# A list scheduler inside a spectral-mixing and expert-retrieval kernel: new transfer costs, work taken by latest time, and six instead of seven units by block products

## The chip, the cores and the metric

The kernel runs on one core of one Trainium2 chip. The metric is the device time of one launch in microseconds (us). The matrix engine (TensorE) is PE in the profile, and its weight loads, which overlap the products, are PEld; VectorE is DVE, ScalarE is ACT, GpSimd is POOL, SyncE is SP. SP does no arithmetic here: its instructions issue DMA transfers, one after the other, and an instruction that waits for a semaphore holds up all those behind it.

## The reference

Two layers follow each other, and each does two steps on x, which has 2048 rows (tokens) of 512 numbers:

```python
x = x + A(layernorm(x))     # a = xn @ Wd_re.T; b = xn @ Wd_im.T; A = Ws_re @ a - Ws_im @ b
x = x + B(layernorm(x))     # q = xn @ w_q (32 heads); scores of q's halves against k1 and k2 (16 keys each);
                            # the best two of each half -> the best two of their four pairs -> softmax g;
                            # out = sum over heads and picks of g * gelu(xn . u[pick]) * v[pick]
```

A is a Fourier transform over tokens and features, of which only the real part is kept: Ws has 2048 x 2048 numbers (real and imaginary part), Wd 512 x 512. B looks up 2 of 256 experts for each of the 32 heads of each token.

## The kernel before, in words

**Numbers.** Each float32 operand of a product is split in two float16 words, a high one (by ACT) and a rest (by DVE), and a product is three matmuls: high by high, rest by high, high by rest. The matrices `c` (from the sequence matrix), `xh`/`xl` (the normalised rows), `dh`/`dl` (the hidden matrix) and `wh`/`wl` (w_q folded with the keys) are such pairs.

**Units.** A layer's A step goes over nine units of output tokens: units 0 to 6 have 256 tokens (two tiles of 128), units 7 and 8 have 128 each. A unit first does the sequence product: for pairs of token tiles `p0` it loads two pieces of the sequence matrix (`raw`, 256 KB each), makes the pair `c`, and multiplies with all of `xh`/`xl` into the accumulators `acc`. `seq_unit` (L899 on) does this directly: 192 matmuls of 512 columns for a unit of 256 tokens, at L1054. `fast_unit` (L717 to L896) does it by block products in the manner of Strassen: seven products in place of eight, 336 matmuls of 256 columns at L815. For this, DVE forms sums of blocks of `raw` (L750, L754, L758), ACT and DVE split 1024 and 768 columns per step instead of 1024, and the sums are stored in DRAM (`sum2d`, L788) and read back as `m` (L884); at the end DVE and ACT join the products (L838, L853). Which units are fast is the table `FAST`, one tuple for each layer. Fast units of layer 0 also store `c` (`sum1d`, L791), and a unit that is fast in both layers loads it in layer 1 (L732 on) and prepares nothing.

**Token tiles.** When a unit's sequence product is complete, each of its tiles goes through `token_tile` (L1082 on): 24 matmuls with `dh`/`dl` (L1162), the row is added and normalised again (L289, L327 to L340), split (`xp`), turned by a transposing DMA (`xt`, L1193), multiplied for scores (L1276, L1281) and for u (L1313); DVE finds the best keys (L1368 to L1411), a second turn (`qd`, L1193) and comparisons with `iota` make one-hot factors `lr`; 32 small matmuls (L1670) sum the softmax weights; four DMAs to DRAM and two back (`gdr`, L1740, L1747) rearrange them; after a weighing by the activations the product is turned (`pl`, L1193) and multiplied by v (L1815, L1819). In layer 0 the row is stored in DRAM (`x2d`, L1870) and read again in layer 1. All these transfers are issued by SP. The last tile of layer 1 takes a path of its own ("fine"), with PE transpositions and shorter pieces, because nothing follows it.

**Order.** Nothing runs in the order of the code. Each step is recorded as an operation of one engine (`Plan.op`, L90) with an assumed duration, the operations it must follow (`after`), those it must merely stand behind (`behind`), the buffers that it takes and frees (`Hold`), and a priority `prio`. `Plan.run` (L97) is a list scheduler: it keeps a clock for each engine, and of the operations that can start first on an engine it takes the one with the least `prio`. The start times give the order in which each engine's instructions are emitted; on the chip each engine then runs its own list in that order and waits by semaphores. A load occupies SP for its whole transfer (`load(kb)` is 1.05 us for 256 KB) and lands `lag` 2.3 us later; a transposing DMA is `TURN, TURNED = 1.2, 1.4`. In the tail, after the last sequence product, PE is fed idle matmuls (`fill`, L2021) where the plan has a gap of over 0.8 us: they keep it running and compute nothing.

**Set-up.** In the first 160 us w_q is loaded in 32 pieces of 512 KB (`wr`, L529), split (`w`, L603, L271) and folded with the keys by small matmuls (L617, L619), between the sequence products of units 0 to 2. No tile can have its scores before that is complete.

## Time and profile before

| quantity | value |
|---|---|
| three runs | 1168.27, 1174.51, 1174.88 us (median 1174.51) |
| the profiled execution: its time, its span | 1169.87 us, 1168.1 us |
| PE busy, share of the span | 1114.9 us, 95% |
| DVE busy | 1008.0 us, 86% |
| ACT busy | 624.8 us, 53% |
| POOL busy | 56.4 us, 5% |
| the transfers of SP's queue: share of the 16 DMA engines | 58.3% (187.54 MB) |

The page's first part gives busy times, of which the largest is the first guess at a bound. Idle time counts only on the engine that sets the end; on the others it is slack. A wait row reads "engine, line waited for, the engine and line that ended the wait: us in total, times, the longest". A row of the windows view gives, for a stretch of the span, busy us and number of instructions of each engine, the share of full speed that TensorE's clock was granted (PEclk), and the DMA engines' busy share and rate. Rows of the chain and of the timeline begin with start and duration in us. Consecutive matmuls overlap: a 512-column matmul has 379 ns on its own row, and the next starts 216 ns after it, so a rate is read from a run of them.

### The profile page before, as it was taken

How to read it: one execution, taken by the hardware profiler on the slowest of the kernel's cores; microseconds unless marked ns; L12 is line 12 of the kernel's file. 1: busy time of each engine (PE TensorE's matmuls, PEld its weight loads, DVE VectorE, ACT ScalarE, POOL GpSimd, SP SyncE). 2: the span in 40 equal slices, each digit the busy share in tenths (PEclk: the TensorE clock that was granted, in tenths of full speed). 3: DMA queues.
4: the chain of work that ended last, by engine and by line, in shares of the span. 5: the costliest groups of instructions: out<-in, count | busy, mean ns of one | idle time of the engine just before them, and what ended most of it. 6: DMA issues, size and time to landing. Idle time of an engine off the chain costs nothing.

```text
span 1168.1 us, 21993 instructions
## 1 busy us (share of the span) xinstructions
PE 1114.9 (95%) x8350; PEld 687.0 (59%) x8350; DVE 1008.0 (86%) x2048; ACT 624.8 (53%) x1200; POOL 56.4 (5%) x106
## 2 busy tenths in 40 slices
PE   8999999989999879999999999999999899999996
PEld 3345544444458556766645644667776666667574
DVE  8768879998799998989896589999999977988696
ACT  6666666566555465556654575654644345344322
POOL 2100000001000000000000000000000000000000
PEclk9999999999999999999999999999999999999998
DMA  8688764455367877644536442787687765454111
GB/s 275 200 265 270 252 214 107 129 131 132 105 178 237 197 240 196 198 108 104 157 97 145 152 113 90 209 214 204 203 211 238 176 164 131 126 107 112 32 29 31
DMA packets 307587, 189.16 MB, mean 162 GB/s; under 512 B 193424, under 2 KB 267408, under 8 KB 307472
## 3 DMA queue, kind: packets, MB, share of 16 engines
q1 hardware_dynamic: 307328, 187.54, 58.3%
q8 instruction: 67, 1.10, 0.4%
q14 instruction: 48, 0.39, 0.1%
q10 hardware_dynamic: 144, 0.13, 0.0%
HBM read 137.77 MB, written 36.57 MB: 149 GB/s over the span
## 4 chain that ended last, share of the span: by engine, by line
PE 48%; DVE 29%; DMA 11%; ACT 4%; issue 4%; SPq 3%; POOL 1%; DVEq 0%; ACTq 0%
PE acc L1054 13%; PE acc L815 10%; PE bank L1162 9%; PE bank L1276 5%; DVE c L271 4%; PE bank L1281 3%; DVE eq L1390 3%; DMA raw<-in_cseq 3%; DVE eq L1368 2%; DMA xt<-xp 2%; PE bank L1313 2%; DVE lr L1634 2%; DVE tmp L1374 2%; DVE tmp L1381 1%; PE bank L1815 1%
## 5 line engine op out<-in xcount | busy, mean ns | idle before, releaser
L1054 PE MATMUL acc<-c,xh 128*128 128x512 f16 (+1 forms) x1232 | 327.1, 346 | 3.3 <-DVE ptl L271 2.2
L1054 PE MATMUL acc<-c,xl 128*128 128x512 f16 (+1 forms) x616 | 213.0, 346 | 1.9 <-DVE xl L405 1.9
L1054 PEld LDWEIGHTS <-xh 128*128 128x128 f16 x1360 | 133.0, 98 | 106.8 <-DVE ptl L271 2.2
L277 ACT ACTIVATE c<-raw 128x1024 f16<-128x1024 f32 (+1 forms) x120 | 118.9, 995 | 67.5 <-PE acc L1054 26.4
L271 DVE SCALAR_TENSOR_TENSOR c<-raw,c 128x1024 f16<-128x1024 f32 (+1 forms) x120 | 137.3, 1148 | 11.8 <-ACT c L277 10.9
L1162 PE MATMUL bank<-dh,pth 128*128 128x512 f16 (+1 forms) x264 | 97.7, 373 | 0.5 <-ACT pth L277 0.5
L815 PEld LDWEIGHTS <-xch 128*128 128x128 f16 x896 | 88.5, 99 | 15.6 <-DMA m<-sum2d 2.2
L1054 PEld LDWEIGHTS <-xl 128*128 128x128 f16 x680 | 66.5, 98 | 52.9 <-DVE xl L405 3.0
L1162 PE MATMUL bank<-dl,pth 128*128 128x512 f16 (+1 forms) x264 | 97.6, 373 | 0.0
L1162 PE MATMUL bank<-dh,ptl 128*128 128x512 f16 (+1 forms) x264 | 92.6, 373 | 0.0
L1276 PE MATMUL bank<-wh,xt 128*128 128x512 f16 x216 | 82.0, 380 | 10.6 <-DMA xt<-xp 10.4
L815 PE MATMUL acc<-c,xh 128*128 128x256 f16 x448 | 85.6, 274 | 6.7 <-ACT c L277 3.3
L1390 DVE SCALAR_TENSOR_TENSOR eq<-eq 128x512 f16<-128x512 f16 x186 | 86.1, 463 | 1.0
L815 PE MATMUL acc<-m,xch 128*128 128x256 f16 x448 | 79.6, 276 | 6.2 <-DMA m<-sum2d 6.2
L815 PE MATMUL acc<-c,xch 128*128 128x256 f16 x448 | 85.1, 275 | 0.0
L1162 PEld LDWEIGHTS <-pth 128*128 128x128 f16 x528 | 50.9, 98 | 52.9 <-ACT pth L277 0.6
L1276 PE MATMUL bank<-wl,xt 128*128 128x512 f16 x216 | 81.9, 379 | 0.0
L1634 DVE TENSOR_TENSOR lr<-iota,qt 128x2048 f16<-128x2048 f16 x58 | 69.5, 1219 | 10.7 <-ACT qt L1601 9.8
L1368 DVE TENSOR_TENSOR eq<-sc,val 128x1024 f16<-128x1024 f32 x62 | 75.8, 1223 | 1.4
L1276 PEld LDWEIGHTS <-xt 128*128 128x128 f16 x432 | 41.1, 98 | 60.5 <-DMA xt<-xp 14.2
L815 PEld LDWEIGHTS <-xh 128*128 128x128 f16 x672 | 65.9, 98 | 13.3 <-issue 3.3
L1281 PE MATMUL bank<-wh,xt 128*128 128x512 f16 x248 | 63.6, 379 | 0.0
(243 smaller groups left out, 2208.8 us busy)
## 6 DMA issues: line engine op xcount, KB each, us to landing
raw<-in_cseq SPq DMA_DIRECT2D x192, 256.0 KB, 3.5
m<-sum2d SPq DMA_DIRECT2D x84, 256.0 KB, 3.6
wr<-in_wq SPq DMA_DIRECT2D x32, 512.0 KB, 5.8
sum2d<-s SPq DMA_DIRECT2D x40, 384.0 KB, 3.5
sum1d<-c SPq DMA_DIRECT2D x16, 512.0 KB, 3.7
raw<-in_ctile SPq DMA_DIRECT2D x32, 256.0 KB, 3.7
c<-sum1d SPq DMA_DIRECT2D x16, 512.0 KB, 4.3
e<-x2d SPq DMA_DIRECT2D x30, 256.0 KB, 3.0
```

The costliest lines, as they stand in the source:

```text
L271: nc.vector.scalar_tensor_tensor(lo, src, scale, hi, op0=ALU.mult, op1=ALU.subtract)
L277: nc.scalar.activation(hi, src, AF.Copy, scale=scale)
L815: nc.tensor.matmul(acc[m][:, dd], w(pw, dd), moving(pm), start=(first and dd == 0 and k == 0), stop=(j == half_t - 1 and dd == 1 and k == ...
L1054: nc.tensor.matmul(target(d), w[:, s, d * P:(d + 1) * P], moving(s % per, part), start=(s == 0 and k == 0 and d % blocks == 0), stop=(s == ...
L1162: nc.tensor.matmul(t["y", cs.start], w[:, k, c, t0:t0 + P], r[:, c, k, cs], start=(z == 0 and c == 0 and m == 0), stop=(z == len(steps) - ...
L1276: nc.tensor.matmul(t["pc", hf], t["th"][:, k, :], r[:, k, hf], start=(k == 0 and r is wh), stop=False, skip_group_check=fine)
L1281: nc.tensor.matmul(t["pc", hf], t["tl"][:, k, :], wh[:, k, hf], start=False, stop=(k == KD - 1), skip_group_check=fine)
L1313: nc.tensor.matmul(t["xu"], w[:, k, :], r[:, k, :], start=(m == 0), stop=(m == 3 * KD - 1))
L1368: nc.vector.tensor_tensor(t["eq"][:, :, cols], flat("sc")[:, :, cols], val(rank_, cols), op=ALU.is_equal)
L1374: nc.vector.tensor_max(t["tmp"][:, :, cols], flat("sc")[:, :8, cols], flat("sc")[:, 8:, cols])
L1390: nc.vector.scalar_tensor_tensor(s[:, :m], s[:, :m], 2.0 ** m, s[:, m:2 * m], op0=ALU.mult, op1=ALU.max)
L1634: nc.vector.tensor_tensor(both(r), iota[:, :, 0:4][:, None, :, :].to_broadcast([P, 32, E, 4]), rows(r), op=ALU.is_equal)
```

## The change

The change has four parts.

- **Costs.** A transfer now has three numbers: the time for which it occupies its issuer, its share of a common pipe, and a tail until it has landed. `load` becomes 0.5, 0.98 us per 256 KB, 1.55; the new `store` 0.48, 0.84 per 256 KB, 1.05; the transposing DMA of `xt` 1.3, 1.55, 1.4, those of `qd` and `wt` (the `pl` row) 1.3, 0.65, 1.4; the `gdr` transfers 0.7, 0.13, 1.6 and 0.7, 0.96, 1.5. Transfers pass the common pipe one after the other.
- **Choice.** The plan is made 8 times. After each pass, `latest` works a latest start for every operation back from the start times of PE's operations, every second time with PE's operations packed without gaps; in the next pass DVE, ACT, POOL and SP take the operation with the least latest time. PE still goes by `prio`. The pass with the earliest end is kept.
- **Units.** `FAST` goes from ((5, 6), (2, 3, 4, 5, 6)) to ((6,), (1, 2, 3, 5, 6)): six block-product units instead of seven. Unit 4 is a direct unit in both layers; layer 0 stores its `c` (`keptd`, L1079 of the new program) and layer 1 loads it, without a split by ACT and DVE. The order of layer 1's units goes from 0, 7, 1, 2, 3, 4, 5, 6, 8 to 0, 7, 4, 3, 6, 1, 2, 5, 8.
- **Queue and small waits.** The `x2d` stores of layer 0 are issued by ACT instead of SP. Some operations get a further predecessor (`last[i][0]`, `p_place`, `first_m`, `setup_done`) which their data needs or which stood ahead anyway.

```diff
-FAST = ((5, 6), (2, 3, 4, 5, 6))
+FAST = ((6,), (1, 2, 3, 5, 6))
+KEPT = (4,)
...
+        self.issue = None
+        if isinstance(us, tuple):
+            self.issue, us, lag = us
...
+    def best(self, passes):
+        found, due = None, None
+        for k in range(passes):
+            out = self.run(due)
+            end = max(o.end for o in out)
+            if found is None or end < found[0]:
+                found = end, [(o.start, o) for o in out]
+            due = self.latest(out, k % 2)
...
+    def latest(self, out, packed):
...
+        for o in sorted(out, key=lambda o: o.start):
+            if o.engine == "PE":
+                t = due[o.n] = o.start if t is None or not packed else t
+                t += o.us
+        for o in sorted(out, key=lambda o: -o.start):
+            own = o.us + o.lag + (o.issue or 0.0)
+            d = min([t + 3.0 - own] + [due[n] - (own if whole else 0.0) - 0.1 for n, whole in follow.get(o.n, ())])
+            due[o.n] = min(due.get(o.n, d), d)
...
-                    t, o = min((c for c in can if c[0] <= first + 1e-9), key=lambda c: (c[1].prio, c[1].n))
+                    key = (lambda c: (c[1].prio, c[1].n)) if due is None or e == "PE" else (lambda c: (due[c[1].n], c[1].n))
+                    t, o = min((c for c in can if c[0] <= first + 1e-9), key=key)
...
-            free[e] = t + max(o.us - self.OVER.get(e, 0.0), 0.06 if o.us else 0.0)
-            o.end = t + o.us + o.lag
-            if o.lag:
+            if o.issue is None:
+                free[e] = t + max(o.us - self.OVER.get(e, 0.0), 0.06 if o.us else 0.0)
+                o.end = t + o.us + o.lag
+            else:
+                free[e] = t + o.issue
+                moved = max(moved, t + BEGIN) + o.us
+                o.end = moved + o.lag
...
-TURN, TURNED = 1.2, 1.4
+BEGIN = 0.55
+ROUND = (0.7, 0.13, 1.6), (0.7, 0.96, 1.5)
+TURN = {"xt": (1.3, 1.55, 1.4), "qd": (1.3, 0.65, 1.4), "wt": (1.3, 0.65, 1.4)}
...
 def load(kb):
-    return kb / 256 * 1.05
+    return 0.5, kb / 256 * 0.98, 1.55
+
+
+def store(kb):
+    return 0.48, kb / 256 * 0.84, 1.05
...
-    ORDER = ([0, 1, 2, 3, 4, 5, 6, 7, 8], [0, 7, 1, 2, 3, 4, 5, 6, 8])
+    ORDER = ([0, 1, 2, 3, 4, 5, 6, 7, 8], [0, 7, 4, 3, 6, 1, 2, 5, 8])
...
+            if layer and n in KEPT:
+                def f4():
+                    t["c"] = two_words()
+                    nc.sync.dma_start(t["c"][2], kept_d[KEPT.index(n), p0 // 2])
...
-            moves.append(op("SP", 0.3, f_out, evac[1:], behind=moves[:1], take=[hd] if k == 0 else [], last=[hgs], prio=prio,
-                            lag=2.4))
+            moves.append(op("SP", ROUND[0], f_out, evac[1:], behind=moves[:1], take=[hd] if k == 0 else [], last=[hgs], prio=prio,
+                            ))
...
-            back.append(op("SP", 0.4, f_in, moves + [a_act], behind=back, take=[hgt] if j == 0 else [], last=[hd], prio=prio, lag=3.5))
+            back.append(op("SP", ROUND[1], f_in, moves + [a_act], behind=back, take=[hgt] if j == 0 else [], last=[hd], prio=prio))
...
-        x2done[i] = op("SP", load(256), lambda: nc.sync.dma_start(x2d[i], t["row"]), [a],
-                       last=[] if keep else [hrow], prio=prio, lag=2.3)
+        x2done[i] = op("ACT", store(256), lambda: nc.scalar.dma_start(x2d[i], t["row"]), [a],
+                       last=[] if keep else [hrow], prio=prio)
...
-    order = sorted(plan.run(), key=lambda o: o.start)
+    order = plan.best(8 if narrow else 1)
```

What moves shows only in the emitted lists. Counted over the whole program, PE has 192 more matmuls of 512 columns with `acc`, 336 fewer of 256 columns, and 38 idle matmuls in the tail instead of 22; DVE has four fewer joins `e<-e,acc` and the same number of splits; SP has 16 fewer `x2d` stores (ACT has them), 12 fewer loads of `m`, and 8 stores and 8 loads of `keptd` in the place of 8 and 8 of `sum1d`.

Three places follow, each first as it was. **SP's queue at the end of the set-up** (`wr` is a piece of w_q, `raw` one of the sequence matrix, of which 56 stand ahead of the last w_q piece before, and 50 now):

```order
L529 DMA wr<-in_wq 128x2x512 x7
L972 DMA raw<-in_cseq 128x2x256 x2
L529 DMA wr<-in_wq 128x2x512
L972 DMA raw<-in_cseq 128x2x256 x2
L529 DMA wr<-in_wq 128x2x512 x3
L972 DMA raw<-in_cseq 128x2x256 x2
L529 DMA wr<-in_wq 128x2x512
L972 DMA raw<-in_cseq 128x2x256 x2
L529 DMA wr<-in_wq 128x2x512
```

```order
L585 DMA wr<-in_wq 128x2x512
L1187 DMA row<-in_x 128x512 x2
L585 DMA wr<-in_wq 128x2x512 x2
L1040 DMA raw<-in_cseq 128x2x256 x2
L585 DMA wr<-in_wq 128x2x512 x3
L1040 DMA raw<-in_cseq 128x2x256 x2
L585 DMA wr<-in_wq 128x2x512 x6
L1040 DMA raw<-in_cseq 128x2x256 x2
L585 DMA wr<-in_wq 128x2x512 x2
```

The w_q pieces come with fewer `raw` loads between them, and the last one comes after six fewer of those.

**SP's queue in layer 0, among the token tiles** (`x2d<-row` stores a finished row, the transposing DMAs turn `xp`, `q` and `ph`):

```order
L1193 DMA_TRANSPOSE qd<-q 128x3x128
L744 DMA raw<-in_cseq 128x2x256 x2
L1193 DMA_TRANSPOSE pl<-ph 128x4x128
L1870 DMA x2d<-row 128x512
L1114 DMA row<-in_x 128x512
L791 DMA sum1d<-c 128x2048
L1870 DMA x2d<-row 128x512
L1193 DMA_TRANSPOSE xt<-xp 128x8x128
```

```order
L1266 DMA_TRANSPOSE qd<-q 128x3x128
L1820 DMA g_3062<-gdr 64x16x16 x2
L505 DMA e_3077<-in_x 128x512
L505 DMA e_3084<-in_x 128x512
L1040 DMA raw<-in_cseq 128x2x256 x2
L1187 DMA row<-in_x 128x512
L1079 DMA keptd<-c 128x2048
L1266 DMA_TRANSPOSE pl<-ph 128x4x128
L1266 DMA_TRANSPOSE xt<-xp 128x8x128
```

Before, a turn could stand behind two row stores; now there are none in SP's queue, and the new store of `c` stands there.

**DVE in the tail**, where the last tile's row is normalised (`stats`, `picks`, `xn`) beside the work of the tile ahead of it (`lr`, `eq`):

```order
L346 BN_AGGR stats<-e_13887 128x2
L349 TENSOR_SCALAR stats<-stats 128x1
L352 TENSOR_SCALAR picks<-stats 128x1
L355 TENSOR_SCALAR picks<-picks 128x1
L1206 TENSOR_SCALAR xn<-row,stats,picks 128x256
L358 TENSOR_SCALAR stats<-stats,picks 128x1
L1206 TENSOR_SCALAR xn<-row,stats,picks 128x256
L1390 SCALAR_TENSOR_TENSOR eq<-eq 128x128
```

```order
L402 BN_AGGR stats<-e_13714 128x2
L1722 TENSOR_TENSOR lr<-iota,qt 128x1024
L405 TENSOR_SCALAR stats<-stats 128x1
L1722 TENSOR_TENSOR lr<-iota,qt 128x1024
L408 TENSOR_SCALAR picks<-stats 128x1
L1732 TENSOR_TENSOR lr<-lr,qt 128x1024
L411 TENSOR_SCALAR picks<-picks 128x1
L1722 TENSOR_TENSOR lr<-iota,qt 128x1024
L1279 TENSOR_SCALAR xn<-row,stats,picks 128x256
L414 TENSOR_SCALAR stats<-stats,picks 128x1
L1732 TENSOR_TENSOR lr<-lr,qt 128x1024
L1279 TENSOR_SCALAR xn<-row,stats,picks 128x256
```

The six `lr` instructions of the tile ahead stood behind the normalisation; now five stand between the row's sum and the first `xn` (one of them ahead of the rows shown), and the sixth ahead of the second.

More of the change, by code (lines that the diff above doesn't have):

```diff
@@ L115, in run @@
                     names = [h.pool for h in o.take]
-                    spare = [(sorted(self.pools[n]), names.count(n)) for n in set(names)]
+                    spare = [(sorted(x[0] for x in self.pools[n]), names.count(n)) for n in set(names)]
                     if all(len(p) >= c for p, c in spare):
@@ L150, in run @@
                              (u.late if a.engine != "PE" else 0.0) for a in u.after] +
-                            [a.start + a.us for a in u.behind])
+                            [a.start + (a.us if a.issue is None else a.issue) for a in u.behind])
                     ready[u.engine].append((r, u))
@@ L744, in f0 @@
                     nc.sync.dma_start(dst, cseq[n, :, 2 * j + z].rearrange("c p t -> p c t"))
[L746 removed]
+                loads.append(op("SP", load(256), f0, [], take=[] if z else [hr], behind=loads[-1:], prio=(0,) + turn + (z,)))
             def f1():
@@ L967, in joint @@
             turn = rank + (next(turns),)
+            if layer and n in KEPT:
+                def f4():
+                    t["c"] = two_words()
+                    nc.sync.dma_start(t["c"][2], kept_d[KEPT.index(n), p0 // 2])
+                a = op("SP", load(512), f4, [keptdone[n, p0]], take=[hc], behind=corder[-1:], prio=(0,) + turn)
+                corder.append(a)
+                cdone[layer, n] = a
+                for y in range(2):
+                    high[p0 + y] = a
+                    joined[p0 + y] = (a, hc, lambda q, part, y=y: of(t["c"][part][:, 512 * y:512 * y + 512], q))
+                return
             for z in range(2):
@@ L1008, in joint, with f5 @@
             cdone[layer, n] = b1
+            if layer == 0 and n in KEPT:
+                def f5():
+                    nc.sync.dma_start(kept_d[KEPT.index(n), p0 // 2], t["c"][2])
+                keptdone[n, p0] = op("SP", store(512), f5, [b1, c1], last=[hc], prio=(0,) + turn + (2,))
         def target(d):
@@ L1114, in row @@
             nc.sync.dma_start(t["row"], x_in[i * P:(i + 1) * P, :] if layer == 0 else x2d[i])
-        a_row = op("SP", load(256), row, ([x2done[i]] if layer else []) + [near[layer, n]], take=[hrow], prio=prio, lag=2.3)
+        a_row = op("SP", load(256), row, ([x2done[i]] if layer else []) + [near[layer, n]], take=[hrow], prio=prio)
         a = None
@@ L1844, in token_tile @@
                 queue, issuer = (nc.sync, "SP") if z == 0 else (nc.scalar, "ACT")
-                stores.append(op(issuer, load(128), lambda cs=cs, queue=queue: queue.dma_start(
-                    out[i * P:(i + 1) * P, cs], t["row"][:, cs]), [a], last=[hrow], prio=prio, lag=2.3))
+                stores.append(op(issuer, store(128), lambda cs=cs, queue=queue: queue.dma_start(
+                    out[i * P:(i + 1) * P, cs], t["row"][:, cs]), [a], last=[hrow], prio=prio))
             return
@@ L1864, in token_tile @@
         if layer:
-            stores.append(op("SP", load(256), lambda: nc.sync.dma_start(out[i * P:(i + 1) * P, :], t["row"]), [a],
-                             last=[hrow], prio=prio, lag=2.3))
+            stores.append(op("SP", store(256), lambda: nc.sync.dma_start(out[i * P:(i + 1) * P, :], t["row"]), [a],
+                             last=[hrow], prio=prio))
             return
```

85 lines of the change are left out of this document (53 added, 32 removed).

## Prediction

> **What bounds the kernel now.** I read the page's first part, then TensorE's own waits, then the stretches in which it idles.
>
> ```profile
> PE 1114.9 (95%) x8350; PEld 687.0 (59%) x8350; DVE 1008.0 (86%) x2048; ACT 624.8 (53%) x1200; POOL 56.4 (5%) x106
> ```
>
> PE is busy for 95% of the 1168.1 us span: no change of order gains more than the other 53.2 us, and work added to PE costs its full time. The windows view says where those lie (its columns: stretch, length, then busy us of PE, PEld, DVE, ACT, POOL, the granted clock, DMA share, GB/s):
>
> ```profile
> 0.00:50.00 50.00, 44.29 (x189) 18.81 (x190) 41.26 (x108) 34.80 (x52) 12.92 (x38) 1.00 0.75 242
> 50.00:650.00 600.00, 574.86 (x4245) 335.94 (x4244) 518.44 (x1007) 346.53 (x651) 31.54 (x32) 1.00 0.61 173
> 650.00:1100.00 450.00, 437.39 (x3342) 292.54 (x3341) 393.67 (x799) 222.96 (x434) 11.06 (x35) 1.00 0.60 158
> 1126.00:1168.00 42.00, 32.38 (x344) 19.36 (x341) 29.72 (x82) 9.39 (x27) 0.85 (x1) 0.92 0.16 32
> ```
>
> PE idles 5.7 us at the start, 25.1 in layer 0, 12.6 in layer 1 and 9.6 in the tail. The waits view names what ended the idle times:
>
> ```profile
> PE bank L1276 <- DMA xt<-xp: 10.4, 10, 1.9
> PE acc L815 <- DMA m<-sum2d: 6.4, 4, 2.7
> PE bank L1815 <- DMA pl<-ph: 5.3, 4, 2.1
> ```
>
> These three, all transfers, are 22.1 of the 37.7 us in the middle. No single wait rules; there are many stops of 1 to 2 us where the order expected something earlier than it came. That is the place of this change.
>
> **The change part by part.** *Block products (a).* One unit of 256 tokens goes from 336 matmuls of 256 columns to 192 of 512. Two undisturbed runs in the chain give the rates:
>
> ```profile
> 349.46 14.41 PE acc L815 x132
> 710.18 20.07 PE acc L1054 x93
> ```
>
> 14.41/132 = 0.1092 us and 20.07/93 = 0.2158 us, so 192 x 0.2158 - 336 x 0.1092 = 41.4 - 36.7: **+4.7 us**, on the bound and certain.
>
> *Turns by DMA (b).* The old plan gives each 1.2 + 1.4 = 2.6 us. The transfers view, with median us from issue to landing last:
>
> ```profile
> xt<-xp SPq DMA_TRANSPOSE x27, 3.3
> qd<-q SPq DMA_TRANSPOSE x27, 2.4
> pl<-ph SPq DMA_TRANSPOSE x27, 2.7
> ```
>
> For `xt` it was 0.7 us short, and PE's stops there have a mean of 10.4/10 = 1.0. The new figure is 0.55 + 1.55 + 1.4 = 3.5. A stop that is due to a wrong figure shrinks by 0.9: about 3 of the 10.4 are left, **-7.4**. Bounds: -10.4, and 0 if the tiles' cover shrinks. Counted along PE's order at the two rates, the work between a tile's last product with `dh` and its first score product is 12.4 us at the least before and 12.7 now; it is under 18 us for 12 of 27 tiles before and 13 now. So cover is no larger; only its use can be better.
>
> *The second fast unit of layer 0 (c).* PE's timeline has four stops in a row where unit 6 begins, right behind unit 5:
>
> ```profile
> 421.75 0.69 PE L1670 MATMUL bank<-lr 128*64 128x64 f16 x32 [1.90 <-DVE lr L1638]
> 429.69 0.38 PE L815 MATMUL acc<-c,xh 128*128 128x256 f16 x2 [1.73 <-DVE c L271]
> 435.52 0.27 PE L815 MATMUL acc<-c,xh 128*128 128x256 f16 x1 [3.27 <-ACT c L277]
> 437.10 0.38 PE L815 MATMUL acc<-c,xh 128*128 128x256 f16 x2 [1.20 <-DVE c L271]
> 437.50:440.90 3.40, 3.40 (x18) 2.41 (x17) 3.40 (x8) 1.85 (x2) 0.00 (x0) 0.50 0.69 239
> ```
>
> 8.1 us of idling, and behind the 3.27 us stop the clock is at half speed for 3.4 us, which costs 1.7 more: 9.8. DVE is the cause, by the mean ns of the preparation's instructions:
>
> ```profile
> L271 DVE SCALAR_TENSOR_TENSOR c<-raw,c 128x1024 f16<-128x1024 f32 x104 | 126.4, 1219 | 10.8 <-ACT c L277 10.7
> L271 DVE SCALAR_TENSOR_TENSOR s<-raw,s 128x768 f16<-128x768 f32 x40 | 37.7, 951 | 3.4 <-ACT s L277 3.4
> L750 DVE TENSOR_TENSOR raw<-raw 128x512 f32<-128x512 f32 x40 | 27.3, 686 | 3.0 <-DMA raw<-in_cseq 2.8
> L754 DVE TENSOR_TENSOR raw<-raw 128x256 f32<-128x256 f32 x40 | 16.4, 418 | 0.0
> L758 DVE TENSOR_TENSOR raw<-raw 128x256 f32<-128x256 f32 x40 | 16.4, 418 | 0.0
> ```
>
> A prepared fast unit takes 8 x (1.219 + 0.951 + 0.686 + 0.418 + 0.418) = 29.5 us of DVE, a direct one 8 x 1.219 = 9.8. Layer 0 loses one of its two prepared units, 19.8 us of DVE, and unit 6 now follows a direct unit. I take three quarters: **-7.5** (-9.8 to 0).
>
> *Waits for `m` (d).* Four stops, 6.4 us; the longest is followed by half clock again:
>
> ```profile
> 1072.76 0.37 PE L815 MATMUL acc<-m,xch 128*128 128x256 f16 x1 [2.74 <-DMA m<-sum2d]
> 1072.40:1075.80 3.40, 3.04 (x15) 2.17 (x15) 0.85 (x2) 1.18 (x2) 0.00 (x0) 0.50 0.45 108
> ```
>
> With six fast units in place of seven, and transfers that share a pipe in the plan: **-3** of 8.1 (-8.1 to 0). The Trainium skill (TensorE: Matmul & The Clock Gate, "Why this matters for your kernels") puts the drop of the clock at idle gaps of over some 3 us. The 3.27 us stop agrees, the 2.74 us stop lies below; if that drop had another cause, its 1.7 us would stay, (d) would be -1.3 and the sum below -10.5.
>
> *SP's queue (e).* The old plan lets SP spend 0.3 us on a `gdr` store and 0.4 on the load back, and 1.05 on a load; by the trace SP is held otherwise:
>
> ```profile
> L1740 SPq DMA_DIRECT2D gdr<-lr x124: 576/631/1624, 239.9 to 1146.3; - x124
> L1747 SPq DMA_DIRECT2D g<-gdr x62: 585/647/1787, 245.3 to 1150.8; - x62
> L1870 SPq DMA_DIRECT2D x2d<-row x16: 319/338/563, 259.2 to 645.4; - x16
> SPq L1870 <- DVE row L289: 8.4, 4, 4.0
> SPq L1870 <- DVE tmp L1381: 8.1, 1, 8.1
> ```
>
> The new figures, 0.7 and 0.5, are near 0.63, 0.65 and 0.34. The `x2d` stores go to ACT: 16 x 0.338 = 5.4 us of its time, and whatever they wait there. Behind one on ACT stand evacuations (`lr<-bank`, `junk<-row`), the latter waiting for the same row anyway. ACT idles 47% of the span, so I cost it at nothing; uncovered, it is the 16.5 us of SP's waits above, on ACT instead. From the shorter queue I take half of the `pl` stops: **-2.5** (-5.3, or +3 if ACT's waits hold up its evacuations).
>
> *The rest of the middle (f),* 37.7 - 22.1 - 8.1 = 7.5 us of small stops: **-2** (-7.5, or +3 if new ones come).
>
> *DVE in layer 1 (g).* It gets the 19.8 us: four prepared units (3, 1, 2, 5) for three. Its row has 393.7 of 450 us busy, 87%; with the added work 92%. The three prepared ones now stand last, 1, 2, 5 without a light unit between. **+3** (0 to +10, half the added work).
>
> *Set-up (h).* Counted as above, PE's last folding product stands 135.3 us of PE work from the start, and 149.6 before: 14.3 earlier. Six `raw` loads less ahead of the last w_q piece, 1.57 MB, bring its landing forward by 6 us at 260 GB/s. PE was already at the edge there:
>
> ```profile
> PE bank L619 <- DVE w L271: 0.6, 2, 0.4
> 30.00:40.00 10.00, 8.52 (x40) 3.61 (x38) 9.13 (x25) 8.15 (x13) 2.69 (x4) 1.00 0.56 177
> 40.00:50.00 10.00, 9.37 (x44) 4.06 (x43) 6.49 (x13) 6.60 (x9) 1.06 (x2) 1.00 0.65 211
> 50.00:60.00 10.00, 9.59 (x45) 4.31 (x44) 5.83 (x12) 5.03 (x7) 0.00 (x0) 1.00 0.64 205
> 150.00:160.00 10.00, 9.63 (x88) 4.96 (x85) 6.92 (x9) 5.35 (x7) 0.00 (x0) 1.00 0.87 260
> ```
>
> So PE may wait for up to 14.3 - 6 = 8.3 us, unless the pipe, whose share was only 0.56 to 0.65 between 30 and 60 us, is filled earlier. At 260 GB/s there it would carry (83 + 49 + 55) x 10 us = 1.9 MB more, 7 us. **+2** (0 to +8.3). The Trainium skill (DMA: Bandwidth & Descriptors, "Specifications") gives about 358 GB/s as the limit of a core's HBM traffic; by that the set-up has room, (h) is 0 and the sum -14.2.
>
> *Tail (i).* Five `lr` instructions of some 0.63 us (the row below has three in 1.90) now stand ahead of `xn`, which PE waits for: +3.2. But they no longer stand ahead of the search for the best keys:
>
> ```profile
> 1133.59 0.41 DVE L1206 TENSOR_SCALAR xn<-row,stats,picks 128x256 f32<-128x256 f32 x1
> 1137.66 1.90 DVE L1649 TENSOR_TENSOR lr<-iota,qt 128x1024 f16<-128x1024 f16 x3 [0.95 <-ACT qt L1601]
> 1140.68 0.68 DVE L1434 TENSOR_REDUCE val<-acc 128x32 f32<-128x512 f32 x1
> 1136.95 1.03 PE L1281 MATMUL acc<-wh,xt 128*128 128x512 f16 x4
> ```
>
> `val` began at 1140.7 though its scores were there at 1138.0; those 2.7 us come back. **+0.5** (-2 to +3). The 16 added idle matmuls fill time that is lost anyway.
>
> **The sum.** +4.7 - 7.4 - 7.5 - 3 - 2.5 - 2 + 3 + 2 + 0.5 = -12.2. The profiled execution took 1169.9 us (1.8 outside the span), so it would take 1157.7. It lies 4.6 below the median of the three runs; counted from that median, 1174.5, it is 1162.3. I take the middle, **1160.0 us**, 14.5 below the median. The start (5.7 us) and what follows PE's last product stay.
>
> **The rivals.** *Later work, more stops (slower).* DVE, ACT and SP now take the most urgent work first, so work with time left is done just before it is due, and each delay reaches PE. Place: L1276 and L1815 of the new program's tiles. For it: 13 tiles have under 18 us of cover. Price: stops of 1.9 (the longest at `xt`) and 1.3 (5.3/4, the mean at `pl`) at each of these 13 are 41.6 us for 15.7 now, +25.9; without (b) and (e) the sum is -2.3, so +23.6, by the same middle 1196; with half the added stops +10.7, 1183. It decides once the two kinds of stops exceed 18 us together. Against it: the durations in the plan are nearer the trace's.
>
> *No difference.* The gain in layer 0 is given back: DVE binds in units 1, 2, 5 (+10 for +3) and the set-up stops PE for 8.3. That is -12.2 + 7 + 6.3 = +1.1, some 1173. For it: DVE at 92%; against it, DVE's idle time, 13.6 us, in the stretch where the prepared unit 2 now comes:
>
> ```profile
> 950.00:1000.00 50.00, 48.89 (x371) 30.65 (x369) 36.39 (x75) 21.31 (x46) 1.72 (x2) 1.00 0.61 153
> ```
>
>
> *All stops go.* The lower bounds of (b) to (f) are -41; with three quarters of that, the +4.7 and (g) to (i) as forecast the sum is -20.6, some 1152.
>
> *The change does not do what it says:* the first pass, by priority, could have been the best. The mixed `lr` and `stats` rows in DVE's order speak against it; I give it nothing.
>
> **How the numbers follow.** Forecast 0.50, all stops go 0.16, no difference 0.19, later work 0.15. A measurement tells about 1% (11.7 us) from no change, so faster means under 1162.8 and slower over 1186.3. Of the forecast I count 0.41 as faster and 0.09 as within; all stops is faster; of no difference 0.02 each is faster and slower, 0.15 within; of later work 0.12 is slower. Faster 0.59, same 0.27, slower 0.14. The forecast's own range is 1148 to 1170. For 8 in 10 it reaches down to 1140, into the case of all stops, and up to 1184, through that of no difference into the half price of later work.
>
> **What would show it.** Right: PE busy near 1120 us; waits at `xt` near 3 us; no half clock near unit 6 of layer 0; PE idle in the middle near 25 us; DVE over 90% in layer 1. Wrong: waits for `xt`, `pl` and `lr` at or over their old sums; a block of idle PE before the last folding product near 140 us; stops on `c` in the last three prepared units; DVE waiting less while PE waits more.

## The result, and the profile after

The changed kernel takes **1154.6 us** (median of 4 runs, 1153.9 to 1157.6), the kernel before 1174.7 (4 runs, 1168.3 to 1175.2). The ratio is **0.9846 with a 95% interval of [0.9808, 0.9885]**: faster by 1.5%. The forecast was 1160.0 us, the range 1140 to 1184.

The profiled execution took 1154.0 us, with a span of 1152.2 after 1168.1. The page's first part:

```profile
PE 1118.7 (97%) x8222; PEld 673.5 (58%) x8222; DVE 998.1 (87%) x2044; ACT 621.3 (54%) x1196; POOL 50.0 (4%) x106
```

PE has 3.8 us more work and 19.7 us less idle time (33.5 for 53.2). Where, the windows view says, with the stretches of the prediction but for the tail, which now begins earlier:

```profile
0.00:50.00 50.00, 47.23 (x208) 20.65 (x209) 45.63 (x118) 39.98 (x59) 12.95 (x38) 1.00 0.88 286
50.00:650.00 600.00, 588.61 (x4169) 327.75 (x4167) 502.75 (x981) 339.83 (x645) 23.55 (x32) 1.00 0.61 165
650.00:1100.00 450.00, 441.13 (x3425) 298.19 (x3423) 414.03 (x854) 230.79 (x464) 12.60 (x35) 1.00 0.62 158
```

PE idles 2.8 us at the start (5.7 before), 11.4 in layer 0 (25.1), 8.9 in layer 1 (12.6): the gain lies in layer 0 above all. The waits of PE, with the sum, the number and the longest:

```profile
PE acc L871 <- DMA m<-sum2d: 6.2, 5, 2.7
PE bank L1888 <- DMA pl<-ph: 3.5, 1, 3.5
PE bank L1349 <- DMA xt<-xp: 3.0, 3, 1.5
```

The three transfers that stopped PE for 22.1 us now do so for 12.7. The stops at `xt` have shrunk, those at `m` have not.

A second cut is free of the question what counts as idle: the moment at which the last sequence product with `acc` begins. The view of one line's instructions has it (duration in ns, least, median, most; then first and last start), first of before and then of after:

```profile
L1054 PE MATMUL acc<-c,xh x1232: 272/379/390, 23.2 to 1126.1; 128*128 128x512 f16 x121, 128*128 128x256 f16 x55
```

```profile
L1127 PE MATMUL acc<-c,xh x1360: 272/379/390, 22.9 to 1107.4; 128*128 128x512 f16 x139, 128*128 128x256 f16 x56
```

Up to there the program is 18.7 us shorter; from there to the end it takes 44.8 us after 42.0, 2.8 longer. I call the two parts the *middle* and the *tail* below.

### The profile page after: what moved, and what is told of

Its sections match the earlier page's. It is cut to its first block, busy times and chain, and to the rows that moved or that the text cites. A ratio compares the mean times of both kernels' runs of the same rounds, so it can differ in the third digit from the quotient of the medians.

```text
span 1152.2 us, 21748 instructions
## 1 busy us (share of the span) xinstructions
PE 1118.7 (97%) x8222; PEld 673.5 (58%) x8222; DVE 998.1 (87%) x2044; ACT 621.3 (54%) x1196; POOL 50.0 (4%) x106
## 4 chain that ended last, share of the span: by engine, by line
PE 55%; DVE 27%; DMA 8%; issue 4%; ACT 3%; SPq 1%; POOL 0%; DVEq 0%; ACTq 0%
PE acc L1127 22%; PE bank L1235 10%; PE bank L1349 6%; PE acc L871 5%; DVE c L327 3%; PE bank L1354 3%; DVE eq L1463 2%; DVE eq L1441 2%; DMA m<-sum2d 2%; DVE lr L1707 2%; PE bank L1386 2%; PE bank L1127 2%; DMA xt<-xp 2%; DVE ptl L327 1%; DVE tmp L1447 1%
## 5 line engine op out<-in xcount | busy, mean ns | idle before, releaser
L1127 PE MATMUL acc<-c,xh 128*128 128x512 f16 (+1 forms) x1360 | 366.0, 349 | 2.4 <-DVE ptl L327 2.4
L1127 PE MATMUL acc<-c,xl 128*128 128x512 f16 (+1 forms) x680 | 237.3, 349 | 0.0
L1127 PEld LDWEIGHTS <-xh 128*128 128x128 f16 x1488 | 145.5, 98 | 118.1
L1127 PEld LDWEIGHTS <-xl 128*128 128x128 f16 x744 | 72.8, 98 | 60.1 <-issue 3.6
L871 PEld LDWEIGHTS <-xch 128*128 128x128 f16 x768 | 75.5, 98 | 10.5 <-DMA m<-sum2d 0.4
L871 PE MATMUL acc<-c,xh 128*128 128x256 f16 x384 | 72.6, 273 | 2.6 <-DVE e L909 1.6
L871 PE MATMUL acc<-c,xch 128*128 128x256 f16 x384 | 72.4, 273 | 0.0
L871 PE MATMUL acc<-m,xch 128*128 128x256 f16 x384 | 67.1, 275 | 3.6 <-DMA m<-sum2d 3.4
L339 ACT ACTIVATE sc<-bank 128x512 f32<-128x512 f32 x62 | 36.0, 592 | 49.9 <-PE bank L1354 25.8
```

What stands on the lines that cost most here:

```text
L339: nc.scalar.activation(dst, src, AF.Copy, scale=scale)
L871: nc.tensor.matmul(acc[m][:, dd], w(pw, dd), moving(pm), start=(first and dd == 0 and k == 0), stop=(j == half_t - 1 and dd == 1 and k == ...
L1127: nc.tensor.matmul(target(d), w[:, s, d * P:(d + 1) * P], moving(s % per, part), start=(s == 0 and k == 0 and d % blocks == 0), stop=(s == ...
```

## The experiments

The theories, by the letters that the expectations use: **A**, the gain comes from the costs, which are nearer the trace; **B**, from the choice by latest time in eight passes; **C**, from the six units and their order; **D**, row stores on ACT cost time there; **E**, whatever one plan brings over another like it is chance of the order; **F**, the new figures for `sum2d` and `m` are too short. Every kernel is the changed program with something put back; all are timed against before on the same chip. The runs lie on three chips, on which before took 1167.8, 1171.1 and 1169.3 us, so from one run to another the ratios are to be compared. Two things were put back in several of them:

```diff
-FAST = ((6,), (1, 2, 3, 5, 6))
-KEPT = (4,)
+FAST = ((5, 6), (2, 3, 4, 5, 6))
+KEPT = ()
-    ORDER = ([0, 1, 2, 3, 4, 5, 6, 7, 8], [0, 7, 4, 3, 6, 1, 2, 5, 8])
+    ORDER = ([0, 1, 2, 3, 4, 5, 6, 7, 8], [0, 7, 1, 2, 3, 4, 5, 6, 8])
```

These are the *old units*. The *old costs* are the old figures and the `x2d` stores on SP:

```diff
-ROUND = (0.7, 0.13, 1.6), (0.7, 0.96, 1.5)
-TURN = {"xt": (1.3, 1.55, 1.4), "qd": (1.3, 0.65, 1.4), "wt": (1.3, 0.65, 1.4)}
+ROUND = (None, 0.3, 2.4), (None, 0.4, 3.5)
+TURN = {"xt": (None, 1.2, 1.4), "qd": (None, 1.2, 1.4), "wt": (None, 1.2, 1.4)}
...
-    return 0.5, kb / 256 * 0.98, 1.55
+    return None, kb / 256 * 1.05, 2.3
...
-        x2done[i] = op("ACT", store(256), lambda: nc.scalar.dma_start(x2d[i], t["row"]), [a],
+        x2done[i] = op("SP", store(256), lambda: nc.sync.dma_start(x2d[i], t["row"]), [a],
```

With both put back and one pass, the program gives the instruction lists of before nearly line for line, so the other small edits should not matter; no run timed that program.

### One part at a time, in the first three kernels, and two of them in the fourth

**costs_only**: new costs, old units (as above), one pass by priority.

```diff
-    order = plan.best(8 if narrow else 1)
+    order = plan.best(1)
```

> The new transfer costs (and the row stores on ACT) alone: one pass by priority, seven fast units and the unit order as before. Theory A, the forecast's (the plan's transfer times were wrong, PE's stops at xt and pl come from that): a ratio to before of 0.990 (0.985 to 0.994), PE's waits at xt near 3 us for 10.4, the stops where unit 6 of layer 0 begins still there. Theory B (the choice by latest time is what helps, better costs without it change little): 0.998 to 1.003, waits at xt near 10. Theory C (fewer fast units and their order are what helps): the same 0.998 to 1.003.

Measured: 1171.3 us, ratio 1.0027 [1.0008, 1.0045]. PE's waits:

```profile
PE acc L871 <- DMA m<-sum2d: 9.0, 8, 2.5
PE acc L871 <- DVE e L909: 8.1, 5, 2.1
PE bank L1743 <- DVE lr L1711: 7.5, 4, 3.0
PE bank L1349 <- DMA xt<-xp: 3.8, 1, 3.8
```

The stops at `xt` fall from 10.4 to 3.8 us, as Theory A has it, and nothing is gained: the stops at `m`, at the joins `e` and at `lr` have grown to 24.6 us (10.1 before: 6.4, 0.5 and 3.2). Theory A falls. The row stores on ACT are in this run too, but at the 1.6 to 3.2 us that emit_act gives them below they do not hide a gain of 1%.

**units_only**: new units; old costs (as above), one pass.

```diff
-    order = plan.best(8 if narrow else 1)
+    order = plan.best(1)
```

> Six fast units, unit 4's c kept, the new order of layer 1; costs as before (row stores on SP), one pass by priority. Theory C: 0.985 to 0.990, since the 9.8 us at the second fast unit of layer 0 and its waits for m go, against 4.7 us more of TensorE work. Theory A: 0.998 (the 7.5 us gained there against 4.7 us of work and 3 us in layer 1), waits at xt still near 10 us. Theory B: 1.000 to 1.006.

Measured: 1170.9 us, ratio 1.0036 [1.0014, 1.0058]. That hides two large parts. Here are its window of layer 0, its last sequence product and, from DVE's timeline, the last tile's row `xn` and the search `val` in its scores:

```profile
50.00:650.00 600.00, 587.96 (x4162) 326.70 (x4161) 504.61 (x981) 341.84 (x645) 26.83 (x32) 1.00 0.60 166
```

```profile
L1128 PE MATMUL acc<-c,xh x1360: 272/379/390, 23.5 to 1116.0; 128*128 128x512 f16 x139, 128*128 128x256 f16 x56
```

```profile
1123.27 0.41 DVE L1280 TENSOR_SCALAR xn<-row,stats,picks 128x256 f32<-128x256 f32 x1
...
1126.15 1.21 DVE L1485 SCALAR_TENSOR_TENSOR sc<-eq,sc 128x1024 f32<-128x1024 f16 x1
...
1133.61 1.28 DVE L1508 TENSOR_REDUCE val<-acc 128x32 f32<-128x512 f32 x2
...
1144.38 0.69 DVE L1508 TENSOR_REDUCE val<-acc 128x32 f32<-128x512 f32 x1 [0.24 <-PE acc L1536]
```

PE idles 12.0 us in layer 0, after 25.1, and the middle is 10.1 us shorter than before (1116.0 for 1126.1). But the tail takes 52.9 us after 42.0: 10.9 longer, which is all of it. Between `xn` at 1123.3 and the end of the last search at 1145.1 lie 21.8 us, where before it was 13.1 (1133.59 to 1145.36 + 1.29): DVE does the older tile's work first (`sc` above is a part of it), since by `prio` it is first. The units are worth something, then, that this order loses again.

**choice_only**: eight passes; old units, old costs.

```diff
-KEPT = (4,)
+KEPT = ()
...
-    return 0.5, kb / 256 * 0.98, 1.55
+    return None, kb / 256 * 1.05, 2.3
```

> Eight passes with the choice by latest time; costs, units and order as before. Theory B: 0.985 to 0.990, with stops on DVE's results (lr, c, ptl) and the stops of the first 50 us gone, waits at xt about as before. Theory A: 0.997 to 1.004, since the choice works back from wrong transfer times. Theory C: 1.000.

Measured: 1154.5 us, ratio 0.9893 [0.9858, 0.9927]. Its windows:

```profile
50.00:650.00 600.00, 587.47 (x4330) 344.34 (x4328) 524.10 (x1024) 351.42 (x666) 26.08 (x32) 0.99 0.63 177
650.00:1100.00 450.00, 440.33 (x3392) 298.05 (x3391) 394.29 (x817) 217.83 (x448) 14.92 (x35) 1.00 0.57 152
```

PE idles 12.5 and 9.7 us where it idled 25.1 and 12.6, with nearly the same work on every engine and the same figures. Its stops at `xt` fall to 5.9 us too, where no change was expected. Theory B holds: most of the gain is in the choice.

**costs_choice**: new costs and eight passes; old units.

```diff
-FAST = ((6,), (1, 2, 3, 5, 6))
+FAST = ((5, 6), (2, 3, 4, 5, 6))
```

> New costs and the choice by latest time, but seven fast units in the order as before: the whole change without its units. Theory C: 0.996 to 1.002. Theories A and B: 0.985 to 0.990, at or within 3 us of the whole change, as the units cost 4.7 us of TensorE work and save about 7.5; below the whole change if the stops at unit 6 of layer 0 go by the choice alone.

Measured: 1170.5 us, ratio 1.0010 [0.9985, 1.0035]. With the old units the new costs take away all that the choice brings. This ratio is what Theory C expected, which units_only and choice_only contradict. The loss lies in one stretch, 800 to 900 us; first choice_only, then costs_choice, and the longest stop of the latter:

```profile
800.00:900.00 100.00, 95.76 (x783) 71.88 (x782) 98.12 (x192) 48.66 (x89) 4.41 (x3) 0.98 0.68 192
```

```profile
800.00:900.00 100.00, 84.16 (x724) 64.42 (x723) 90.23 (x180) 47.24 (x85) 2.08 (x2) 0.93 0.75 209
```

```profile
887.56 0.37 PE L871 MATMUL acc<-m,xch 128*128 128x256 f16 x1 [6.50 <-DMA m<-sum2d]
```

PE idles 11.6 us more there and loses 5 us more to the clock (7% of the stretch for 2%). Some 2 us are in both, as the half clock began before two long stops ended; that leaves about 15 of the 20.6 us by which the two spans differ. The releaser is `m`, which is behind 17.5 us in 5 stops over the whole program. The transfers view of costs_choice (median us to landing last):

```profile
m<-sum2d SPq DMA_DIRECT2D x84, 256.0 KB, 4.0
sum2d<-s SPq DMA_DIRECT2D x40, 384.0 KB, 4.5
```

The plan gives the store 2.9 us and the load 3.1. That is Theory F, tried below.

### Two parts at a time, and single figures

**costs_units**: the whole change, but one pass by priority.

```diff
-    order = plan.best(8 if narrow else 1)
+    order = plan.best(1)
```

> The whole change but one pass by priority in place of eight passes with the choice by latest time. Theory A (costs help most, units some, the choice little): 0.985 to 0.989, as the whole change (0.985). Theory B (the choice by latest time is what helps): 0.995 to 1.002, with the start's stops (5.7 us of idling in the first 50 us before, 2.8 in the whole change) back.

Measured: 1182.5 us, ratio 1.0091 [1.0054, 1.0128], slower than before and outside both expected ranges. Its waits on `m` and on the joins are 12.9 us and 7.9 us:

```profile
PE acc L871 <- DMA m<-sum2d: 12.9, 8, 4.0
PE acc L871 <- DVE e L909: 7.9, 3, 4.5
```

**choice_units**: the whole change with the old costs.

```diff
-TURN = {"xt": (1.3, 1.55, 1.4), "qd": (1.3, 0.65, 1.4), "wt": (1.3, 0.65, 1.4)}
+TURN = {"xt": (None, 1.2, 1.4), "qd": (None, 1.2, 1.4), "wt": (None, 1.2, 1.4)}
```

> The whole change with the transfer costs as before (and the row stores on SP). Theory A: 0.995 to 1.000, waits at xt near 10 us and at pl near 5. Theory B: 0.985 to 0.990, waits at xt well below 10 us although the plan's figure for it is 0.9 us short.

Measured: 1150.7 us, ratio 0.9821 [0.9803, 0.9839]. The whole gain is there without one of the new figures. PE still waits longer for `xt` than in the changed kernel, to no harm:

```profile
PE bank L1350 <- DMA xt<-xp: 5.9, 6, 1.7
```

**xt_short**: the whole change with the old share of an `xt` turn, nearly.

```diff
-TURN = {"xt": (1.3, 1.55, 1.4), "qd": (1.3, 0.65, 1.4), "wt": (1.3, 0.65, 1.4)}
+TURN = {"xt": (1.3, 0.65, 1.4), "qd": (1.3, 0.65, 1.4), "wt": (1.3, 0.65, 1.4)}
```

> The whole change, but the turn xt has the share of the other two in the plan (0.65 for 1.55), so that it is planned 0.9 us shorter, at the 2.6 us of before. If the forecast's step on the turns is right, PE's waits at xt rise from 3.0 to 8 to 11 us and the ratio to before from 0.985 to 0.990 to 0.992. If the plan's figure for this one turn does not matter (other work hides it, or the whole order shifts as by chance): 0.983 to 0.988, waits at xt under 5 us.

Measured: 1156.7 us, ratio 0.9868 [0.9845, 0.9891]; the stops at `xt` are 5.7 us instead of 3.0:

```profile
PE bank L1349 <- DMA xt<-xp: 5.7, 5, 2.1
```

So the wait rises by less than expected, and the time by no amount that the intervals tell apart. In jitter_act below, where this figure stays, the same wait is 0.9 us; a part of its rise here may be chance as well.

**rowstore_sp**: the whole change, with the `x2d` stores planned and issued on SP.

```diff
-        x2done[i] = op("ACT", store(256), lambda: nc.scalar.dma_start(x2d[i], t["row"]), [a],
+        x2done[i] = op("SP", store(256), lambda: nc.sync.dma_start(x2d[i], t["row"]), [a],
```

> The whole change with the row stores of layer 0 issued by SP again. If the move cost and gained nothing by itself: 0.984 to 0.987. If SP's queue was relieved by it (16.5 us of SP's waits before): 0.988 to 0.992, with waits at pl and for m above the 3.5 and 6.2 us of the whole change. If ACT's waits cost time: below 0.983.

Measured: **1145.2 us** (1144.1 to 1148.0), ratio **0.9783 [0.9761, 0.9805]**: the fastest of all, ahead of both kernels.

```profile
50.00:650.00 600.00, 593.59 (x4206) 331.65 (x4205) 508.12 (x992) 345.37 (x659) 25.86 (x33) 1.00 0.60 165
650.00:1100.00 450.00, 440.67 (x3464) 301.28 (x3462) 416.32 (x852) 227.42 (x454) 13.39 (x34) 1.00 0.62 158
```

```profile
PE acc L871 <- DMA m<-sum2d: 3.3, 4, 1.4
PE bank L1349 <- DMA xt<-xp: 1.9, 2, 1.2
```

PE idles 6.4 us in layer 0 and 9.3 in layer 1, and no stop at these two transfers is over 1.4 us. This plan differs in the whole order, so the run alone does not say that it is ACT's issuing that costs (D).

### What is order, and what is the queue

**emit_act**: the plan of rowstore_sp, with PE's and DVE's lists word for word; only the emitted stores go to ACT.

```diff
-        x2done[i] = op("ACT", store(256), lambda: nc.scalar.dma_start(x2d[i], t["row"]), [a],
+        x2done[i] = op("SP", store(256), lambda: nc.scalar.dma_start(x2d[i], t["row"]), [a],
```

> The kernel of the run rowstore_sp with every list as there (PE's and DVE's word for word), but the 16 row stores of layer 0 are emitted on ACT at the places where that plan had them on SP. If ACT's queue itself costs the 9 us by which the whole change is behind rowstore_sp (theory D): a ratio of 0.984 to 0.987. If the 9 us are the other order that a plan with the stores on ACT happens to give (theory E): 0.976 to 0.980, within 2 us of rowstore_sp.

Measured: 1148.4 us (1145.6 to 1149.5), ratio 0.9823 [0.9797, 0.9849]; the spans are 1143.9 and 1142.3. By its windows layer 0 is the same within 0.5 us:

```profile
50.00:650.00 600.00, 593.07 (x4202) 331.23 (x4200) 506.86 (x990) 345.03 (x658) 23.06 (x33) 1.00 0.60 165
```

ACT's issuing costs 1.6 us between the spans and 3.2 between the medians, whose ranges overlap. The spans of the changed kernel and of rowstore_sp are 9.9 us apart; the other 8.3 of these come with the other order. By the ratios ACT's issuing has more of it, 0.40 of 0.63%. The ratio lies between the two expected ranges and its interval reaches into both, so D and E are not decided; a small price on ACT is likely.

**jitter_act** and **jitter_sp**: the whole change, and rowstore_sp, with a start of transfers in the plan that is 0.01 us later. It leaves every mechanism as it is and puts a large part of DVE's list in another order.

```diff
-BEGIN = 0.55
+BEGIN = 0.56
```

> The whole change with one plan figure, the delay from issue to the start of a transfer, at 0.56 us instead of 0.55. No mechanism is touched, but a third of DVE's list stands in another order. Theory E (part of what single plans differ by is chance of the order): a ratio that differs from the whole change's 0.985 by more than 0.002 and up to 0.008, either way. If orders of one rule come out alike: 0.984 to 0.986.

> The kernel of rowstore_sp with the same 0.56 us for 0.55. Theory E: a ratio that differs from 0.978 by more than 0.002. Theory D or any fixed gain from the stores on SP: 0.977 to 0.980, below jitter_act by 0.006 again.

Measured: 1154.0 us, ratio 0.9865 [0.9839, 0.9891], for 0.9846; and 1149.8 us, 0.9829 [0.9803, 0.9855], for 0.9783. The same rule with a figure that means nothing gives 0.2% and 0.5% of difference, and the spans move by 1.2 and 5.8 us. Single waits move more than that suggests: the stops at `m` go from 6.2 to 8.4 us and from 3.3 to 9.7. The second pair is what Theory E expected, the first just misses its 0.002. Against that, of the pairs SP and ACT (0.9783 and 0.9846, 0.9829 and 0.9865) both favour SP, by 0.4 to 0.6%, which is about the size of these differences: no more than a hint.

**m_costs**: costs_choice with 1 us more for each store of `sum2d` and each load of `m`.

```diff
-            sum2done[n, j] = op("SP", store(384), f8, [a], last=[hs], prio=(0,) + turn + (3,))
+            sum2done[n, j] = op("SP", (0.48, 1.26, 2.05), f8, [a], last=[hs], prio=(0,) + turn + (3,))
...
-            a = op("SP", load(256), f0, [sum2done[n, j] for j in range(2 * y, 2 * y + 2)], take=[hc], behind=morder[-1:],
+            a = op("SP", (0.5, 0.98, 2.55), f0, [sum2done[n, j] for j in range(2 * y, 2 * y + 2)], take=[hc], behind=morder[-1:],
```

> The kernel of costs_choice (seven units as before, ratio 1.001, PE waiting 17.5 us for m) with the plan's tails of the sum2d store and the m load each 1.0 us longer, since the trace has 4.5 and 4.0 us from issue to landing where the plan has 0.55 + 1.26 + 1.05 = 2.9 and 0.55 + 0.98 + 1.55 = 3.1. If the short figures for these two make the new costs fail with seven units (theory F): waits for m under 7 us and a ratio of 0.986 to 0.992. If not: 0.997 to 1.004 with waits for m still over 10 us; with waits for m gone but the ratio above 0.995, the time comes back at other stops.

Measured: 1167.5 us, ratio 0.9976 [0.9953, 0.9999], for 1.0010.

```profile
PE acc L871 <- DMA m<-sum2d: 13.5, 10, 5.5
```

The stops fall from 17.5 to 13.5 us only. That fall and the change of 0.3% are both within what a meaningless figure does. Theory F is neither shown nor excluded as a part; as the whole cause it fails.

### The twelve together

By the ratios, with the costs (and ACT's stores) in the second and fourth row of figures:

| | old units | new units |
|---|---|---|
| one pass, old costs | 1 (before) | 1.0036 |
| one pass, new costs | 1.0027 | 1.0091 |
| eight passes, old costs | 0.9893 | 0.9821 |
| eight passes, new costs | 1.0010 | 0.9846 |
| eight passes, new costs, row stores on SP | | 0.9783 |

The choice brings 1.1% to 2.5% with the old costs or the new units, and 0.2% where new costs meet old units. The units bring 0.7% and 1.6% with the choice and lose 0.4% and 0.6% without it; the 0.7% is little more than the 0.5% that a meaningless figure did. The costs bring nothing in any pair; with the row stores on SP they would bring 0.4%, which a meaningless figure also does.

The profiled executions split into middle and tail, in us, with what the clock cost at most between 50 and 1100 us (the sum over stretches of 1 us of one minus the granted clock, whether PE was busy or not):

| kernel | last sequence product | tail | lost to the clock |
|---|---|---|---|
| before | 1126.1 | 42.0 | 3.4 |
| the change | 1107.4 | 44.8 | 3.4 |
| units_only | 1116.0 | 52.9 | 1.7 |
| costs_units | 1134.4 | 47.3 | 8.6 |
| choice_only | 1106.7 | 44.8 | 5.1 |
| choice_units | 1106.5 | 42.2 | 1.7 |
| costs_choice | 1129.5 | 42.6 | 13.6 |
| rowstore_sp | 1099.0 | 43.3 | 0 |

The units shorten the middle by 10.1 us without the choice. What the choice adds to them is 9.5 us in the middle and the 10.7 us of the tail that units_only lost (52.9 to 42.2). But the two gains do not add up: the choice alone shortens the middle by 19.4 us, and beside it the units bring 0.2 us there and 2.6 in the tail (choice_only to choice_units). The choice has itself two ingredients, the latest time and the pick among eight plans; no run separates them.

## Why the prediction was right, and which of its steps were not

The forecast for the profiled execution was -12.2 us, and its span moved by -15.9. The middle stretch from 50 to 1100 us has 17.4 us less idle time (37.7 to 20.3), and the forecast's terms (b) to (h) sum to -17.4. That agreement is partly luck: the terms are made up otherwise.

- **(a) Block products, +4.7: right as far as shown.** PE's busy time rose by 3.8 us, but that number holds other things too: the 16 added idle matmuls are in it with 3.9 us (5.5 to 9.4), and the faster clock of the tail takes off up to 2.5 (3.4 to 0.9 lost there). The runs choice_only and choice_units, with 35 and 33 idle matmuls, bear the term out better: 1.4 us more busy time and 3.4 less lost to the clock in the middle, 4.8 together.
- **(b) Turns by DMA, -7.4, and (e) SP's queue, -2.5: the step that failed.** The prediction put this gain down to the new figures. The waits did what it said, `xt` 10.4 to 3.0 us and `pl` 5.3 to 3.5. But each of the three parts alone shrinks the stops at `xt`: the figures to 3.8 us, the choice to 5.9, the units to 6.3. The figures alone gain nothing (costs_only), and without them the whole gain is there (choice_units). So the time that I credited to the durations is not theirs. Most of it comes with the choice, which had no term of its own in the sum and stood only in a rival, as a risk. One stop at `pl` is left, and SP's timeline shows what stood ahead of it:

```profile
279.68 1.89 SPq L1266 DMA_TRANSPOSE xt<-xp  x1
281.61 1.96 SPq L1266 DMA_TRANSPOSE pl<-ph  x1
```

```profile
286.72 0.61 PE L1888 MATMUL bank<-vh,pl 128*128 128x512 f16 x1 [3.53 <-DMA pl<-ph]
```

```profile
286.70:290.10 3.40, 3.38 (x9) 1.24 (x10) 0.60 (x1) 0.81 (x1) 0.00 (x0) 0.52 0.03 5
```

  The row `ph` was ready at 278.5 us, but its turn to `pl` stands right behind one of `xt`; each of these two holds SP for 1.9 us where the plan has 1.3, and the product comes 5.1 us after the issue of `pl` began. Then PE has half clock for 3.4 us.
- **(c) The second fast unit of layer 0, -7.5: right, and it is the units' own gain.** The place behind unit 5, 412 to 445 us now:

```profile
412.00:445.00 33.00, 31.46 (x233) 19.89 (x231) 28.99 (x58) 19.87 (x41) 1.10 (x2) 1.00 0.92 222
```

  1.5 us of idle time at full clock, for 8.1 us and 1.7 of clock before. With the choice but the old units, 4.2 us of stops on `c` and 3.4 of clock are still there (choice_only, 424 to 454 us). The units alone take most of layer 0's stops away too (units_only).
- **(d) Waits for `m`, -3: wrong.** 6.2 us after 6.4 (8.4 in jitter_act). The store and the load had 3.5 and 3.6 us from issue to landing before, and have more now:

```profile
m<-sum2d SPq DMA_DIRECT2D x72, 256.0 KB, 4.6
sum2d<-s SPq DMA_DIRECT2D x40, 384.0 KB, 4.1
```

  The round trip is 1.6 us longer (8.7 for 7.1) and 2.8 us above the plan's 5.9. The longest stop, 2.70 us, is followed by half clock as before, so the two drops of the clock in the middle are still two, in other places. The Trainium skill (TensorE: Matmul & The Clock Gate, "Why this matters for your kernels") has the drop behind gaps of over some 3 us; the 3.53 us stop agrees, and 2.70 and 2.74 us were enough here too, though not every stop of that size was (last section); so the 1.7 us belong to (d) as the sum had it.
- **(f) The rest of the middle, -2: nothing of it came.** Of the 20.3 us of idle time, 12.7 are at the three transfers; the other 7.6 are as many as before.
- **(g) DVE in layer 1, +3: too high.** In layer 1 DVE is busy for 414.0 of 450 us, the forecast 92%, and yet PE's idle time falls from 12.6 to 8.9. In units_only, by priority alone, DVE is at 91% there and PE idles 12.8 us, about as long as before:

```profile
650.00:1100.00 450.00, 437.16 (x3362) 294.68 (x3360) 408.18 (x825) 230.22 (x455) 11.80 (x35) 1.00 0.62 161
```

  With the choice and the old costs the units add 1.3 us in this stretch (9.7 to 11.0). So DVE at 92% costs PE little here, and the rival of no difference, which rested on this and on the set-up, goes with it.
- **(h) Set-up, +2, with the start unchanged: wrong, by some 5 us for the better.** No stop of PE at the folding products is left. The pipe carried what I took for a bound, 260 GB/s, and more:

```profile
30.00:40.00 10.00, 10.00 (x48) 4.56 (x47) 9.60 (x26) 9.02 (x16) 2.56 (x4) 1.00 0.91 286
50.00:60.00 10.00, 9.96 (x76) 4.87 (x74) 6.42 (x8) 4.97 (x9) 0.00 (x0) 1.00 1.01 353
```

```profile
L585 SPq DMA_DIRECT2D wr<-in_wq x32: 367/368/792, 44.0 to 132.5; - x32
```

  The last piece of w_q is issued at 132.5 us, 18.4 earlier than the 150.9 of before:

```profile
L529 SPq DMA_DIRECT2D wr<-in_wq x32: 367/401/469, 62.1 to 150.9; - x32
```

  Both the choice and the costs do this: PE is busy for 46.6 us of the first 50 in choice_only and 46.1 in costs_only, for 44.3 in before and units_only. The Trainium skill's 358 GB/s (DMA: Bandwidth & Descriptors, "Specifications") would have put (h) at 0; the measured 353 is just below it.
- **(i) Tail, +0.5: too low, it is +2.8.** DVE's timeline, with the last search of before, and then `xn` and the first and last search of after:

```profile
1145.36 1.29 DVE L1434 TENSOR_REDUCE val<-acc 128x32 f32<-128x512 f32 x2
```

```profile
1117.46 0.41 DVE L1279 TENSOR_SCALAR xn<-row,stats,picks 128x256 f32<-128x256 f32 x1
...
1122.73 0.69 DVE L1507 TENSOR_REDUCE val<-acc 128x32 f32<-128x512 f32 x1 [1.54 <-PE acc L1354]
...
1128.39 1.29 DVE L1507 TENSOR_REDUCE val<-acc 128x32 f32<-128x512 f32 x2
```

  `xn` comes 10.1 us after the last sequence product began, for 7.5 before: the 2.6 us that `lr` costs ahead of it (I had 3.2). The searches end 12.2 us after `xn`, for 13.1: 0.9 comes back, not 2.7. The other 1.1 us come behind the searches.
- **ACT's row stores at nothing: nearly.** They cost 1.6 to 3.2 us by emit_act, where the ranges overlap.
- **The rival of later work and more stops: no.** It decides at 18 us of stops at `xt` and `pl`; there are 6.5.

What stays open: why the new costs take the choice's gain away with seven units by block products (longer figures for `m` restore a part at most, and from choice_only to costs_choice the row stores move to ACT as well), and how much of the differences below 0.5%, the row stores' among them, is chance of the order.

## What to carry to other kernels

In a list scheduler the rule of choice can matter more than the durations: work taken by the latest time that the bounding engine allows brought 1.1% with the old units and 2.1% with the new, by figures of which the one for `xt` was short by a fifth, while better figures under the old rule only moved the stops from one transfer to other places. A wait that shrinks is not yet time won, so a part is to be run alone, and in both settings of the other parts: units that gained 10 us in the middle lost it again in the tail, and beside the choice, with the old costs, they gained next to nothing in the middle. Two plans of one kernel that differ by less than some 0.5%, the most that the two pairs here moved, should be set beside a third in which a figure without meaning has been moved a little, as here by 0.01 us.

## What the runs showed of the hardware

- A stop of PE of 2.70 us was followed by half clock for 3.4 us, which makes it cost 4.4. The length of the stop alone does not decide this: between 50 and 1100 us of the fourteen traces, every stop of over 3.0 us comes with half clock, but only ten of the 22 between 2.0 and 2.8 us do, and some of just under 2.0 as well. Two stops of jitter_sp show both cases; the granted clock was 0.56 from 474.6 to 478.1 us, and 1.00 from 1043.4 to 1046.8:

```profile
474.64 0.85 PE L1743 MATMUL bank<-lr 128*64 128x64 f16 x32 [1.99 <-DVE lr L1711]
1043.38 0.27 PE L871 MATMUL acc<-m,xch 128*128 128x256 f16 x1 [2.74 <-DMA m<-sum2d]
```

- In rowstore_sp, whose longest stop in that part is 1.94 us, nothing is lost to the clock; costs_choice loses up to 13.6 us to it.
- The set-up moved 353 GB/s on one core in the stretch from 50 to 60 us.
- A transposing DMA held SP for 1.20 to 1.26 us by the medians of after, up to 2.4. The two in a row at 279.68 us took 1.9 each, but three in a row from 388.62 us took 1.26, 1.25 and 1.25.
- The round trip of 384 KB stored and 256 KB loaded through DRAM takes 8.7 us by the medians of after.
